# Every fifth streamed weight piece as two DMAs, of 120 and of 8 partitions

## The chip, the cores and the metric

The kernel runs on one core of a Trainium2 chip. The metric is the time of one execution on the device in microseconds; lower is better. All data are bf16, and sums of products are kept in fp32.

## What is computed

Two branches over the same input x (2048 tokens of 640), mixed by a gate for each token:

```python
g = sigmoid((x * gate_w).sum(-1, keepdims=True))
a = A(x, mem0, Wq, Wk, Wv, Wo, seg_len=32)
b = (gelu(x @ w_gate) * (x @ w_up)) @ w_down          # hidden size 1536
return g * a + (1 - g) * b

def A(x, mem0, Wq, Wk, Wv, Wo, seg_len):              # 32 heads of 192, memory of 8 rows
    mem = mem0
    for s in range(n_seg):                            # 64 segments of 32 tokens
        h = concat([mem, x[segment s]])               # 40 rows of 640
        q, k, v = h @ Wq, h @ Wk, h @ Wv              # for 32 heads
        p = softmax(mask(q @ k.T * scale))            # memory rows see all, tokens are causal
        o = (p @ v) @ Wo                              # 40 rows of 640
        mem = o[:8]                                   # goes into the next segment
        outs.append(o[8:])
    return concat(outs)
```

Branch A is a recurrence: segment s+1 cannot start its projections of the memory rows before segment s has ended. Wq, Wk and Wv have 640 x 6144 elements each, Wo has 6144 x 640.

## The kernel before

All work is written out, instruction by instruction, by a small scheduler of the kernel's own (`_Sched`). `S_.add(engine, fns, reads, writes, dma_sem)` puts an operation at the end of an engine's list and notes which regions of memory it reads and writes. From these regions `finalize` works out the semaphore waits: an operation waits for the last writer of what it reads, and for the writer and the readers of what it overwrites. The order on each engine is that of the calls. On TensorE (PE) an operation that needs more than one wait keeps one, and the others are put on the last matmuls of the operation before it (lines 171 to 186). Other engines issue the waits one after the other ahead of the operation (line 201).

The run has three stages. First the dense branch B for all tokens (lines 739 to 771), then the projections of those rows of all segments that do not depend on the memory (line 804, their results are stored to DRAM and read back segment by segment at line 831), then the 64 segments one after the other (`segment`), which take most of the time.

In a segment, PE goes through the list PROG: projections of Q and K (line 871) and of V (line 905) for four groups of eight heads, transposes (line 883), scores (lines 926 and 937), transposes of the softmax (971, 972), products with V (991, 993) and the output projection (line 1020). The weights are cut into *pieces*: a piece of Wq, Wk or Wv is 128 partitions x 1536 elements (3072 bytes in a row, 384 KB), a piece of Wo is 128 partitions x 2 x 640 elements (two rows of 1280 bytes, 320 KB).

All weights together do not fit into the on-chip memory. Most pieces are *resident*: they are loaded once (line 597). The others, 24 in each segment, are *streamed*: each segment loads them anew, spread evenly over the segment by a table of estimated costs. Streamed pieces go into a ring of five slots (B_RING = 5). `piece(seg, key)` is called for each piece in the order of use. For a streamed piece it calls `issue_ring`, which puts a DMA on the list of SyncE (SP), line 549. As the five slots are taken in turn, this DMA waits until the matmuls that read the slot's piece before have ended. Nothing else runs on SP's queue in the recurrent stage, so an issue that waits holds up the issues behind it. Each slot has its own semaphore (`ring0` to `ring4`), and each has one region of the scheduler, `r_ring[slot]`, over all 128 partitions.

The order of the streamed pieces in a segment is Q, K, V pieces first (15 of them), then nine of Wo. `done` is the place of a piece in this order, 0 to 23. The ACT queue issues the other transfers: one for each segment at line 831, and input and output rows once in four segments (line 640).

Of the kernel before, what the change touches and what calls it, by code (L numbers as in the profile page):

```python
# [221 lines left out]
def _build(nc, A_x, A_mem0, A_Wq, A_Wk, A_Wv, A_Wo, seg_len, w_gate, w_up, w_down,  # L222
# [27 lines left out]
    GQ = OW * 2  # L250
# [6 lines left out]
    S_ = _Sched(nc)  # L257
# [66 lines left out]
    ring_off = [j * GQ for j in range(B_RING)]  # L324
    o = wsA_base - wsB_total
# [6 lines left out]
    o = wsA_base  # L332
# [4 lines left out]
    o = ffn_base  # L337
# [4 lines left out]
    def bview(o, nbytes, plo=0, phi=128):  # L342
        return arena[plo:phi, o // 2:(o + nbytes) // 2]
# [4 lines left out]
    def sreg(o, nbytes, plo=0, phi=128):  # L348
        return Rg("sb", o, o + nbytes, plo, phi)
# [100 lines left out]
    def piece_src(key):  # L450
        if key[0] == 3:
            return Wo2[:, 2 * key[1]:2 * key[1] + 2, :]
        m, o_, k = key
        return (Wq2, Wk2, Wv2)[m][:, k, OW * o_:OW * (o_ + 1)]

    def piece_size(key):
        return GO if key[0] == 3 else GQ

    def piece_view(key, o):
        if key[0] == 3:  # L460
            return bview(o, GO).rearrange("p (c n) -> p c n", n=Dm)
        return bview(o, GQ)
# [55 lines left out]
    o = ring_bytes  # L518
# [9 lines left out]
    o = ring_bytes  # L528
# [5 lines left out]
    assert o <= wsA_base - wsB_total  # L534
    r_res = {key: sreg(o, piece_size(key)) for key, o in res_off.items()}
    r_ring = [sreg(o, GQ) for o in ring_off]
    order_index = {key: i for i, key in enumerate(order)}
    stream_pos = {order[i]: k for k, i in enumerate(stream_list)}
    stream_counter = [0]
# [4 lines left out]
    def issue_ring(seg, upto):  # L544
        done = issued.get(seg, 0)
        while done <= upto:
            key = order[stream_list[done]]
            slot = stream_counter[0] % B_RING
            S_.add("sp", lambda e, slot=slot, key=key: e.dma_start(piece_view(key, ring_off[slot]), piece_src(key)),
                   writes=[r_ring[slot]], dma_sem="ring%d" % slot, name="ring s%d p%d" % (seg, done))  # L550
            stream_counter[0] += 1
            ring_of[(seg, key)] = slot
            done += 1
        issued[seg] = done

    def piece(seg, key):
        oi = order_index[key]
        assert oi == last_req.get(seg, -1) + 1, "pieces must be consumed in `order`"
        last_req[seg] = oi
        if seg == 0:  # L560
            load_late(oi + LATE)
        if key in res_off:
            assert slot_class[key] != 1 or order_index[key] <= order_index[late[late_done[0] - 1]]
            return piece_view(key, res_off[key]), r_res[key]
        issue_ring(seg, stream_pos[key])
        slot = ring_of[(seg, key)]
        return piece_view(key, ring_off[slot]), r_ring[slot]
# [75 lines left out]
    def ffn_x_load(blk):  # L643
# [7 lines left out]
           writes=[r_gwr], dma_sem="gwr")  # L651
# [144 lines left out]
    for o_ in range(NOCT):  # L796
        st, rst_ = lst[o_ % 2], r_lst[o_ % 2]
        for m in range(2):
            gs = [left_piece((m, o_, k)) for k in range(KT)]
            for i in range(12):  # L800
# [6 lines left out]
                    name="left o%d m%d c%d" % (o_, m, i))  # L807
# [9 lines left out]
        for d in range(nd):  # L817
            lo, hi = d * NSEG // nd, (d + 1) * NSEG // nd
# [4 lines left out]
                name="left store")  # L823

    issue_ring(0, B_RING - 1)
    S_.add("pool", lambda e: e.memset(pl_sb, 0.0), writes=[r_p])
    S_.add("pool", lambda e: e.memset(Ks[64:128, 8:12, :], 0.0), writes=[r_Kz[0]])
# [251 lines left out]
    for s in range(NSEG):  # L1079
# [6 lines left out]
                ring=B_RING, arena_bytes=arena_bytes,  # L1086
# [25 lines left out]
def bass_gated_mix__memory_aug_recurrent_mem_tr__glu_gated_geglu__prompt_kernel(  # L1112
    nc,
    A_x,
    A_mem0,
    A_Wq,
    A_Wk,
    A_Wv,
    A_Wo,
    A_seg_len,  # L1120
    B_x,
    B_w_gate,
    B_w_up,
    B_w_down,
    gate_w,
    out,
):
    _build(nc, A_x, A_mem0, A_Wq, A_Wk, A_Wv, A_Wo, A_seg_len, B_w_gate, B_w_up, B_w_down, gate_w, out)
# [33 lines left out]
```

## Time and profile before

| | |
|---|---|
| time, median of 3 runs | 2227.48 us (2223.69 to 2227.95) |
| span of the profiled execution, first to last instruction | 2220.5 us |
| time of the profiled execution beside its span | the profile gives the span alone; the median of the runs is 7.0 us above it |
| mean granted TensorE clock | 0.986 |
| PE busy | 1912.3 us (86%) |
| VectorE / ScalarE / GpSimd busy | 943.6 / 799.7 / 273.6 us |
| DMA packets, bytes | 363257, 642.75 MB, 289 GB/s on average |
| HBM read | 618.74 MB |

How to read it: the time of a run is that of the whole execution, and the span is what the hardware profiler saw of it in one further execution. PE is TensorE's matmuls, PEld its weight loads, DVE VectorE, ACT ScalarE, POOL GpSimd, SP SyncE; a q behind the name (SPq) is the engine's sequencer, which issues DMAs and waits. "arena" is the one on-chip buffer in which all tiles lie, "ps" the accumulation banks. The chain of waits is followed back from the last instruction: at each step to what released it. "From issue to landing" of a DMA is the time from its issue on the queue to the last of its semaphore's increments. The 16 DMA engines' share of busy time is a mean over all of them.

### The profile page before, as it was taken

The page shows a single profiled execution, that of the slowest core. Times are in us where ns is not written, and L with a number is a line of the kernel's source. Part 1 is how long each engine was busy: PE and PEld are TensorE (multiplying, and loading weights), DVE is VectorE, ACT ScalarE, POOL GpSimd, SP SyncE. Part 2 cuts the span into 40 slices and gives each one's busy share as a digit, 9 for nine tenths or more (in the row PEclk, how much of TensorE's full clock was granted, in tenths as well). Part 3 has the DMA queues.
Part 4 walks back from the last instruction along what each step waited for, and adds up shares of the span by engine and source line. Part 5 has one row for each costly group of instructions (what it writes and reads, how often), then busy time and mean ns, then how long its engine had stood idle before and what let it go on. Part 6 is the DMA issues. An engine that isn't in the chain of part 4 may idle for free.

```text
span 2220.5 us, 94985 instructions
## 1 busy us (share of the span) xinstructions
PE 1912.3 (86%) x41834; PEld 1231.3 (55%) x41862; DVE 943.6 (42%) x3184; ACT 799.7 (36%) x2248; POOL 273.6 (12%) x1210
## 2 busy tenths in 40 slices
PE   7999958888888888888888888888888888888887
PEld 3544425555555555555565655555555655555655
DVE  2222223444444444444444444444444544444444
ACT  2222223334333333343333333333333334333333
POOL 0000001111111111111111111111111111111111
PEclk9999989999999999999999999999999999999999
DMA  9203579999999999999999999999999999999998
GB/s 370 88 13 112 150 236 331 322 303 316 301 318 307 324 303 311 305 316 312 319 320 311 316 300 320 306 313 310 320 302 321 309 322 311 315 315 316 310 309 278
DMA packets 363257, 642.75 MB, mean 289 GB/s; under 512 B 60498, under 2 KB 231770, under 8 KB 362842
## 3 DMA queue, kind: packets, MB, share of 16 engines
q1 hardware_dynamic: 311770, 601.01, 80.2%
q10 hardware_dynamic: 51072, 35.66, 5.4%
q8 instruction: 327, 5.36, 0.9%
q14 instruction: 88, 0.72, 0.1%
HBM read 618.74 MB, written 17.83 MB: 287 GB/s over the span
## 4 chain that ended last, share of the span: by engine, by line
PE 46%; DMA 32%; DVE 14%; ACT 3%; issue 3%; ACTq 2%; SPq 0%; DVEq 0%
PE ps L871 12%; DMA arena<-in_A_Wv_dram 10%; DMA arena<-in_A_Wo_dram 9%; PE ps L1020 9%; DMA arena<-in_A_Wk_dram 8%; PE ps L905 7%; DMA arena<-in_A_Wq_dram 4%; DVE arena L974 4%; PE ps L804 3%; PE ps L883 2%; PE ps L742 2%; PE ps L739 2%; ACTq L819 2%; PE ps L757 2%; DVE ps L954 2%
## 5 line engine op out<-in xcount | busy, mean ns | idle before, releaser
L871 PE MATMUL ps<-arena 128*32 128x384 bf16 x10240 | 488.1, 330 | 69.6 <-DMA arena<-in_A_Wk_dram 23.6
L1020 PE MATMUL ps<-arena 128*128 128x40 bf16 x15360 | 457.9, 180 | 64.8 <-DVE arena L1007 38.1
L1020 PEld LDWEIGHTS ps<-arena 128*128 128x128 bf16 x15360 | 428.9, 96 | 88.8 <-DVE arena L1007 49.5
L871 PEld LDWEIGHTS ps<-arena 128*32 128x32 bf16 x10240 | 247.1, 97 | 254.6 <-DMA arena<-in_A_Wk_dram 63.2
L905 PE MATMUL ps<-arena 128*32 128x384 bf16 x6400 | 324.4, 331 | 53.3 <-DMA arena<-in_A_Wv_dram 30.2
L877 ACT ACTIVATE arena<-ps 128x384 bf16<-128x384 f32 x512 | 249.8, 488 | 181.0 <-PE ps L871 105.1
L974 DVE TENSOR_TENSOR arena<-ps,arena 128x320 bf16<-128x320 bf16 x256 | 125.8, 491 | 387.0 <-PE ps L972 387.0
L835 POOL COPY arena<-arena 128x96 bf16<-128x96 bf16 x256 | 67.4, 263 | 1665.0 <-PE ps L937 1138.3
L956 ACT ACTIVATE ps<-ps 104x160 f32<-104x160 f32 x256 | 71.9, 281 | 494.5 <-DVE ps L954 494.5
L905 PEld LDWEIGHTS ps<-arena 128*32 128x32 bf16 x6400 | 144.6, 96 | 175.5 <-DMA arena<-in_A_Wv_dram 59.2
L883 PE MATMUL ps<-arena 128*128 128x128 bf16 x1536 | 175.9, 223 | 32.0 <-ACT arena L877 31.9
L1001 ACT ACTIVATE arena<-ps 128x320 bf16<-128x320 f32 x256 | 112.3, 439 | 215.4 <-PE ps L993 213.8
L991 PE MATMUL ps<-arena 128*128 128x160 bf16 (+1 forms) x768 | 130.5, 260 | 57.1 <-DVE arena L977 39.6
L916 ACT ACTIVATE arena<-ps 128x384 bf16<-128x384 f32 x256 | 125.6, 491 | 139.0 <-PE ps L905 138.7
L839 POOL COPY arena<-arena 64x32 bf16<-64x32 bf16 (+1 forms) x768 | 165.4, 215 | 47.3
L883 PEld LDWEIGHTS ps<-arena 128*128 128x128 bf16 x1536 | 88.1, 98 | 135.7 <-ACT arena L877 91.1
L952 DVE TENSOR_REDUCE arena<-ps 104x4 f32<-104x160 f32 x256 | 80.9, 316 | 149.3 <-PE ps L937 149.3
L894 ACT ACTIVATE arena<-ps 64x128 bf16<-64x128 bf16 x512 | 136.8, 267 | 6.3
L887 DVE COPY arena<-ps 128x384 bf16<-128x384 bf16 x256 | 89.4, 349 | 102.0 <-PE ps L883 102.0
L993 PE MATMUL ps<-arena 128*128 128x64 bf16 (+1 forms) x768 | 124.5, 202 | 4.0 <-ACT arena L877 4.0
L958 DVE TENSOR_REDUCE arena<-ps 104x4 f32<-104x160 f32 x256 | 83.1, 325 | 99.8 <-ACT ps L956 99.8
L991 PEld LDWEIGHTS ps<-arena 128*128 128x128 bf16 x768 | 72.3, 97 | 91.2 <-DVE arena L977 90.7
(81 smaller groups left out, 1886.3 us busy)
## 6 DMA issues: line engine op xcount, KB each, us to landing
arena<-in_A_Wo_dram SPq DMA_DIRECT2D x591, 320.0 KB, 4.7
arena<-in_A_Wv_dram SPq DMA_DIRECT2D x398, 384.0 KB, 5.2
arena<-in_A_Wk_dram SPq DMA_DIRECT2D x340, 384.0 KB, 5.3
arena<-in_A_Wq_dram SPq DMA_DIRECT2D x276, 384.0 KB, 5.0
left_qk_scratch<-arena ACTq DMA_DIRECT2D x16, 768.0 KB, 8.7
arena<-left_qk_scratch ACTq DMA_DIRECT2D x64, 192.0 KB, 4.6
arena<-in_A_x_dram SPq DMA_DIRECT2D x4, 640.0 KB, 15.0
ffn_b_scratch<-arena ACTq DMA_DIRECT2D x16, 160.0 KB, 1.8
```

The lines of the kernel that those rows point to most:

```text
L839: S_.add("pool", lambda e, a=a, b=b, lo=lo, hi=hi, sa=sa: e.tensor_copy(out=Ks[lo:hi, a:b, L:R], in_=stg[lo:hi, o, 1, sa:sa + b - a]), rea ...
L871: S_.add("pe", [lambda e, j=j, k=k, g_=g_: e.matmul(ps[32 * j:32 * j + 32, bank, 0:384], Hb[hb][:, k, 0:L], g_[:, 384 * j:384 * (j + 1)], ...
L877: S_.add("act", lambda e: e.activation(out=rows_sb, in_=ps[:, bank, 0:384], func=ACTF.Copy), reads=[r_ps[bank]], writes=[r_rows], name="ro ...
L883: S_.add("pe", [lambda e, c=c: e.transpose(pv[:, c * 128:(c + 1) * 128], rows_sb[:, c * 128:(c + 1) * 128], ident) for c in range(3)], rea ...
L894: S_.add("act", lambda e, a=a, lo=lo: e.activation(out=Ks[lo:lo + 64, a:a + 4, 0:L], in_=src[lo:lo + 64, 1], func=ACTF.Copy), reads=[r_ps[ ...
L905: return [lambda e, j=j: e.matmul(ps[32 * j:32 * j + 32, bk, 0:384], lhs, g_[:, 384 * j:384 * (j + 1)], start=(k == 0), stop=(k == KT - 1) ...
L916: S_.add("act", lambda e: e.activation(out=v_sb[o % NVB], in_=ps[:, bank, 0:384], func=ACTF.Copy), reads=[r_ps[bank]], writes=[r_v[o % NVB ...
L974: S_.add("dve", lambda e: e.tensor_tensor(out=PTm, in0=apx(pv[:, 512:616], [[64, 2], [0, 4], [1, R]]), in1=apx(mbd, [[0, 2], [1, 4], [0, R]]),
L991: return [lambda e: e.matmul(full, v[:, e0:e0 + 128], PTm[:, ia:ib], start=True, stop=False, skip_group_check=True), lambda e: e.matmul(pa ...
L993: lambda e: e.matmul(part, vl[:, e0:e0 + 128], PTl[:, ia:ib], start=False, stop=True, skip_group_check=True)]
L1001: S_.add("act", lambda e: e.activation(out=apx(u[:, 0, 0, :], [[2 * R, 2], [3 * R, 4], [1, R]]), in_=ps[:, A, 0:2 * W].rearrange("p (c t r ...
L1020: fns.append(lambda e, g_=g_, i=i, c=c, n=n, tl=tl, cc=cc, u=u: e.matmul(ps[:, OB, n * R:(n + 1) * R], g_[:, i, n * 128:(n + 1) * 128], u[ ...
```

## The change

Inside a segment, the streamed pieces whose place `done` leaves 2 when divided by 5 (the places 2, 7, 12, 17 and 22) are issued as two DMAs one after the other: partitions 0 to 119, and partitions 120 to 127. Each slot has two more regions for these parts, and one more semaphore (`ringb0` to `ringb4`) for the second part. The matmuls that use such a piece read the region of the whole slot, so they wait for both. The other pieces, the residents, and the pieces that the stage before the segments streams (line 585) are issued as before. In the 64 segments this makes 320 DMAs more.

```diff
     r_ring = [sreg(o, GQ) for o in ring_off]
+    r_ringp = [(sreg(o, GQ, 0, 120), sreg(o, GQ, 120, 128)) for o in ring_off]
...
             slot = stream_counter[0] % B_RING
-            S_.add("sp", lambda e, slot=slot, key=key: e.dma_start(piece_view(key, ring_off[slot]), piece_src(key)),
-                   writes=[r_ring[slot]], dma_sem="ring%d" % slot, name="ring s%d p%d" % (seg, done))
+            if done % 5 == 2:
+                parts = ((0, 120, r_ringp[slot][0]), (120, 128, r_ringp[slot][1]))
+            else:
+                parts = ((0, 128, r_ring[slot]),)
+            for lo, hi, rg in parts:
+                S_.add("sp", lambda e, slot=slot, key=key, lo=lo, hi=hi: e.dma_start(
+                    piece_view(key, ring_off[slot])[lo:hi], piece_src(key)[lo:hi]),
+                    writes=[rg], dma_sem=("ring%d" if lo == 0 else "ringb%d") % slot, name="ring s%d p%d" % (seg, done))
             stream_counter[0] += 1
```

## The prediction

> **What bounds the kernel now.** I read the page from the top: busy shares, DMA queues, chain of waits; then the longest pieces in order of time, the stages, the lines that issue the pieces, and the waits of PE and of SP.
>
> ```profile
> span 2220.5 us, 94985 instructions
> PE 1912.3 (86%) x41834; PEld 1231.3 (55%) x41862; DVE 943.6 (42%) x3184; ACT 799.7 (36%) x2248; POOL 273.6 (12%) x1210
> ...
> PE 46%; DMA 32%; DVE 14%; ACT 3%; issue 3%; ACTq 2%; SPq 0%; DVEq 0%
> PE ps L871 12%; DMA arena<-in_A_Wv_dram 10%; DMA arena<-in_A_Wo_dram 9%; PE ps L1020 9%; DMA arena<-in_A_Wk_dram 8%; PE ps L905 7%; DMA arena<-in_A_Wq_dram 4%; DVE arena L974 4%; PE ps L804 3%; PE ps L883 2%; PE ps L742 2%; PE ps L739 2%; ACTq L819 2%; PE ps L757 2%; DVE ps L954 2%
> ```
>
> PE is busy most of the time, but the chain that ended last runs through it for 46% only. 32% of it are DMAs, nearly all of them the four streams of weights. So neither is the bound alone: they take turns.
>
> ```profile
> 1000.00:1400.00 400.00, 346.94 (x8547) 233.31 (x8543) 181.19 (x638) 153.11 (x449) 55.87 (x248) 0.99 0.94 314
> 1400.00:1800.00 400.00, 344.73 (x8556) 231.47 (x8553) 184.43 (x654) 152.87 (x449) 56.85 (x252) 1.00 0.93 312
> ```
>
> Two stages of the recurrent loop: PE 346.94 of 400 us, the granted clock full, the 16 DMA engines 93 to 94% busy (the last two columns are their share and GB/s). There is little free time on either side.
>
> ```profile
> 1004.18 5.26 DMA arena<-in_A_Wq_dram
> 1009.44 0.04 issue
> 1009.49 1.32 PE ps L871 x28
> ```
>
> This is one leg of the chain: a piece is issued at 1004.18, lands 5.26 us later, and the projection that had waited for it starts at once. The issue itself had waited for PE to release the slot. Whatever lengthens the landing of such a piece lengthens the span.
>
> ```profile
> L549 SPq DMA_DIRECT2D arena<-in_A_Wo_dram x576: 367/368/1632, 334.2 to 2208.4; - x192
> L549 SPq DMA_DIRECT2D arena<-in_A_Wv_dram x384: 327/328/1191, 262.4 to 2197.9; - x192
> L549 SPq DMA_DIRECT2D arena<-in_A_Wk_dram x320: 327/328/2005, 262.0 to 2195.4; - x160
> L549 SPq DMA_DIRECT2D arena<-in_A_Wq_dram x256: 327/328/1382, 249.1 to 2194.6; - x128
> ...
> DMA to landing us min/median/max: 2.6/5.0/10.1
> ...
> L831 ACTq DMA_DIRECT2D arena<-left_qk_scratch x64: 320/326/2826, 310.0 to 2176.0; - x64
> ```
>
> L549 issues 1536 pieces in 64 segments, 24 in each. L831 issues once a segment, 63 times from 310.0 to 2176.0, so a segment takes 29.62 us and a piece comes every 1.23 us. With a landing of 5.0 us about four pieces (5.0/1.23) are in flight at a time, of the five that the ring holds: half of the landing time is queueing, since the shortest landing is 2.6 us.
>
> **The timed runs.** The page has no time of the profiled execution other than its span, 2220.5 us. The median of the runs is 2227.48, 7.0 us above it; I add changes of the span to the median. About 0.2% (4.5 us) is what a measurement of this kernel can tell from no change.
>
> **The change, part by part.** In each segment the pieces 2, 7, 12, 17 and 22 of 24 come as two DMAs: 320 in all, three of five being weights of Q, K or V (rows of 3072 bytes), two of Wo (two rows of 1280 bytes per partition). Bytes, matmuls and evictions stay the same. Three things are added.
>
> *First, rows on the DMA engines.* A 128-row piece is 8 rows on each of 16 engines. 120 rows do not divide by 16, and the 8 rows of the rest can fall on at most 8 engines. So some engines have between 8 rows (nothing added) and 9 (one added). A row's price is in the queue's row for the stage 600:2100:
>
> ```profile
> q1 hardware_dynamic: 233925, 448.32, 89.0%
> ```
>
> 89.0% of 16 engines over 1500 us are 21360 engine-us for 448.32 MB: 0.146 us for 3072 bytes and 0.122 for 2 x 1280. One row more in each split piece is then 3 x 0.146 + 2 x 0.122 = 0.68 us per segment on the engines that have it, 0.137 on average per split piece. Against 26.4 us (89.0% of 29.62) that these engines work on the ring in a segment, it is 2.6% more.
>
> How much of it reaches the end? If these engines bounded every segment, 64 x 0.68 = 44 us: the upper bound. By the chain it is less: 32% of 2220.5 are 711 us, or 142 legs of 5.0 us. In each leg four pieces are in flight, of which 4.05 x 5/24 = 0.84 are split, so a leg grows by 0.115 us where the engine that finishes last has a ninth row, and by nothing where it has not: between 0 and 16.4 us. No view tells which of the 16 finishes last; I take the middle, 8.2 us, since at most half of the engines have the ninth row and the profile singles none of them out.
>
> [...]
>
> *Second, issues on SP.* 320 more DMA instructions. The trace has small ones at the start:
>
> ```profile
> L649 SPq DMA_DIRECT2D arena<-in_A_mem_dram x1: 397/397/397, 0.8 to 0.8; - x1
> L650 SPq DMA_DIRECT2D arena<-in_gate_w_dram x1: 261/261/261, 1.3 to 1.3; - x1
> ```
>
> These carry 8 and 5 rows and take 0.40 and 0.26 us, about as long as a whole piece. 320 of them are 83 to 128 us of SP. What is queued behind each is the next piece's wait and issue, and behind that PE. What hides it:
>
> ```profile
> SPq L549 <- PE ps L905: 225.7, 183, 2.8
> SPq L549 <- PE ps L871: 215.1, 228, 2.1
> SPq L549 <- PE ps L1020: 176.7, 204, 2.1
> ...
> SPq L549 <- PE ps L883: 58.1, 83, 1.2
> ```
>
> SP waits for PE to release a slot, 1.23, 0.94, 0.87 and 0.70 us on average in these groups, which is longer than one issue. Where the cover fails, the next piece is issued up to 0.40 us late, 128 us at the very most. The chain gives SPq 0%, that is under 0.5% or 11 us for 1536 issues; a fifth more of them is worth about 2 us, and I take that. The second part also starts later than the first by one issue. With four pieces in flight it queues behind rows that are still to be moved, so I put that at nothing; without a queue the piece would land up to 0.40 us late, which for the 0.21 of legs that end on a split piece is 142 x 0.21 x 0.40 = 12 us.
>
> *Third, waits on PE.* A split piece has two semaphores, so PE waits twice, 320 waits more; one of them sits on the matmul before. What is queued behind is the matmul of the piece, which needs both parts anyway. The step "issue" after a landing is 0.04 us in the leg above: 320 x 0.04 = 13 us at most, nothing if the wait rides on an instruction that is issued anyway. I take nothing, since these waits resolve while PE still works on resident pieces in most cases.
>
> Sum: 8.2 + 2 + 0 = about 10 us. 2227.48 + 10 = **2237.5 us**, slower by 0.45%.
>
> **Rivals.** *Nothing measurable.* PE's own idle time for these pieces is small:
>
> ```profile
>   PE ps L871: 40.5, 70
>   PE ps L905: 30.2, 43
> ...
>   PE ps L1020: 23.2, 43
> ```
>
> That is 94 us in 156 waits of the 2220.5. If the split pieces are mostly those that land early, or if the engine with the ninth row has caught up before it matters, the time stays at 2227.5. For it: the 6 to 7% of free engine time, 1.9 us per segment, is more than 0.68. Against: 142 legs in the chain, so the landing decides often.
>
> *Faster.* 120 rows at 8 each fill 15 engines and leave one out. If that one is behind the others throughout now, it loses 5/24 of its ring rows, 0.84 pieces in each leg, and the pieces land when the next slowest is done. The gain has its limit in the 94 us above; a quarter of that, since the next engine takes over, is 23 us and gives 2204. From that point on, at which the left-out engine is more than the added 0.115 us per leg behind, this mechanism decides. For it: a further row of the queues,
>
> ```profile
> q8 instruction: 327, 5.36, 0.9%
> ```
>
> which is 14% of a single engine (0.9% of 16) if all the instruction loading ran on one. Against: nothing shows that it is one, nor which. [...]
>
> *Much slower.* If the 120 rows fall on only 8 engines (15 rows each, plus one), a split piece has 8 rows more on these than now: 8 x 0.68 = 5.5 us per segment against 1.9 us free, 3.6 x 64 = 230 us, or 2457. Half of that unevenness would give about 2280. Against: no row of before, since no ring piece of it has fewer than 128 rows. [...]
>
> **How the numbers follow.** Forecast (slower, up to the bound of 44 us): 0.68. Nothing measurable: 0.14. Faster: 0.11. Much slower: 0.07. So faster 0.11, same 0.14, slower 0.75. The range is from 2223 (the case of no change with its scatter; the fastest run shown is 2223.69) to 2272 (2227.5 plus the bound of 44 us); it leaves out the rivals on both sides, 0.18 together.
>
> **What would show it.** Right: landings of the ring pieces longer by about 0.1 us in the median, DMA waits of PE a little above 94 us, the DMA share at or above 0.93 in the two stages, SPq still near 0% of the chain, GB/s down by about 0.5%. The first step is wrong if the landings are unchanged or shorter, the second if SP's waits for PE vanish at many issues and SPq appears in the chain, the third if "issue" grows by more than 13 us. The whole is wrong if landings fall below 5.0 us and PE waits less for them (the left-out engine was the late one), or if landings of split pieces grow by a microsecond or more (uneven spread).

## The result and the profile after

The changed kernel takes 2400.13 us (median of 4 runs, 2388.53 to 2404.29) against 2225.64 us before (4 runs, 2223.69 to 2227.95): slower by 7.84%, with a 95% interval of 7.54 to 8.14%. My forecast was 2237.5 us and the range ended at 2272. The sign was right, and the size was off by a factor of seventeen: 175 us in place of 10.

The page after, its span, busy shares and chain:

```profile
span 2396.1 us, 95333 instructions
PE 1999.3 (83%) x41862; PEld 1244.6 (52%) x41862; DVE 943.5 (39%) x3184; ACT 800.1 (33%) x2248; POOL 273.6 (11%) x1210
...
DMA 52%; PE 34%; DVE 9%; ACTq 2%; issue 2%; ACT 2%; SPq 0%; DVEq 0%
DMA arena<-in_A_Wk_dram 19%; DMA arena<-in_A_Wv_dram 16%; DMA arena<-in_A_Wo_dram 15%; PE ps L878 7%; PE ps L912 6%; PE ps L1027 6%; PE ps L811 3%; DVE arena L981 3%; PE ps L749 2%; PE ps L746 2%; ACTq L826 2%; PE ps L764 2%; DMA arena<-in_A_Wq_dram 2%; PE ps L890 1%; PE ps L998 1%
```

The span grew by 175.6 us (2396.1 - 2220.5). The chain was 46% PE and 32% DMA; now it is 34% PE and 52% DMA. SPq is still at 0%, so the 320 further issues are not what is late.

The stages (the last two columns are the share of the 16 DMA engines and GB/s), and the ring's queue in the stage 600:2100 (packets, MB, share of 16 engines):

```profile
1000.00:1400.00 400.00, 331.83 (x7748) 213.11 (x7744) 162.97 (x576) 138.85 (x407) 50.07 (x222) 0.99 0.98 285
1400.00:1800.00 400.00, 333.36 (x7774) 215.34 (x7767) 167.21 (x592) 141.10 (x414) 52.35 (x232) 0.97 0.97 286
```

```profile
q1 hardware_dynamic: 216118, 410.37, 93.0%
```

The engines are busier than before (0.97 to 0.98 against 0.93 to 0.94) and move less (285 GB/s against 313). 93.0% of 16 engines over 1500 us are 22320 engine-us for 410.37 MB, which is 0.167 us for a row of 3072 bytes. Before it was 0.146. Each row became 14% dearer on average, though only one piece in five is split. The 8.85 MB of ring pieces in a segment (15 of 384 KB, nine of 320) take 8.85 x (22320/410.37 - 21360/448.32) / 16 = 3.7 us more on each engine. The line that runs once in a segment, now L838, gives a segment's length:

```profile
L838 ACTq DMA_DIRECT2D arena<-left_qk_scratch x64: 320/326/2748, 310.8 to 2347.9; - x64
```

It is (2347.9 - 310.8) / 63 = 32.33 us in place of 29.62, and 64 times 2.72 us are 174. So the 3.7 us account for nearly all of the loss: of free engine time there were about 2 us in a segment (7% of 29.62) and 0.8 us are left (2.5% of 32.33), and the other 2.5 us lengthen the segment.

Who waits for the ring, from the line that issues the pieces (now L555), and the landings of pieces of each size (KB, median us from issue to landing):

```profile
  PE ps L878: 100.0, 181
  PE ps L912: 56.9, 103
...
  PE ps L1027: 34.1, 84
...
DMA to landing us min/median/max: 2.9/5.7/11.8
```

```profile
arena<-in_A_Wv_dram SPq DMA_DIRECT2D x334, 384.0 KB, 6.0
...
arena<-in_A_Wk_dram SPq DMA_DIRECT2D x212, 384.0 KB, 5.9
arena<-in_A_Wk_dram SPq DMA_DIRECT2D x128, 360.0 KB, 6.0
```

The pieces of Wk before:

```profile
arena<-in_A_Wk_dram SPq DMA_DIRECT2D x340, 384.0 KB, 5.3
```

PE now waits 191 us for pieces, 94 before. The split pieces (360 KB is their 120-row part; the view gives no landing for the 8-row part) land about when the whole ones beside them do: all pieces in the queue are late together. That alone does not tell a ninth row on some engines from a higher price of every row, since in both cases the pieces queued behind would be late too. PE's busy time grew as well, by 87 us, with the same matmuls. A matmul of L871, now L878, takes 333 ns on average in place of 330 and the granted clock is 0.979 in place of 0.986, both changes under 1%, so that a slower PE explains at most 20 us of the 175.

### The profile page after: what moved, and what is told of

It is laid out like the page before. It is cut to its first block, busy times and chain, and to the rows that moved or that the text cites. A ratio compares the mean times of both kernels' runs of the same rounds, so it can differ in the third digit from the quotient of the medians.

```text
span 2396.1 us, 95333 instructions
## 1 busy us (share of the span) xinstructions
PE 1999.3 (83%) x41862; PEld 1244.6 (52%) x41862; DVE 943.5 (39%) x3184; ACT 800.1 (33%) x2248; POOL 273.6 (11%) x1210
## 4 chain that ended last, share of the span: by engine, by line
DMA 52%; PE 34%; DVE 9%; ACTq 2%; issue 2%; ACT 2%; SPq 0%; DVEq 0%
DMA arena<-in_A_Wk_dram 19%; DMA arena<-in_A_Wv_dram 16%; DMA arena<-in_A_Wo_dram 15%; PE ps L878 7%; PE ps L912 6%; PE ps L1027 6%; PE ps L811 3%; DVE arena L981 3%; PE ps L749 2%; PE ps L746 2%; ACTq L826 2%; PE ps L764 2%; DMA arena<-in_A_Wq_dram 2%; PE ps L890 1%; PE ps L998 1%
## 5 line engine op out<-in xcount | busy, mean ns | idle before, releaser
L878 PE MATMUL ps<-arena 128*32 128x384 bf16 x10240 | 535.6, 333 | 129.7 <-DMA arena<-in_A_Wk_dram 77.1
L1027 PE MATMUL ps<-arena 128*128 128x40 bf16 x15360 | 476.9, 180 | 73.6 <-DVE arena L1014 35.3
L1027 PEld LDWEIGHTS ps<-arena 128*128 128x128 bf16 x15360 | 438.3, 96 | 107.4 <-DMA arena<-in_A_Wo_dram 48.6
L878 PEld LDWEIGHTS ps<-arena 128*32 128x32 bf16 x10240 | 249.1, 97 | 365.7 <-DMA arena<-in_A_Wk_dram 158.6
L912 PE MATMUL ps<-arena 128*32 128x384 bf16 x6400 | 341.8, 332 | 75.8 <-DMA arena<-in_A_Wv_dram 56.9
L890 PEld LDWEIGHTS ps<-arena 128*128 128x128 bf16 x1536 | 88.5, 98 | 130.3 <-ACT arena L884 63.5
L998 PEld LDWEIGHTS ps<-arena 128*128 128x128 bf16 x768 | 72.8, 98 | 86.8 <-DVE arena L984 86.3
```

Of the source, the lines that this page charges most:

```text
L878: S_.add("pe", [lambda e, j=j, k=k, g_=g_: e.matmul(ps[32 * j:32 * j + 32, bank, 0:384], Hb[hb][:, k, 0:L], g_[:, 384 * j:384 * (j + 1)], ...
L890: S_.add("pe", [lambda e, c=c: e.transpose(pv[:, c * 128:(c + 1) * 128], rows_sb[:, c * 128:(c + 1) * 128], ident) for c in range(3)], rea ...
L912: return [lambda e, j=j: e.matmul(ps[32 * j:32 * j + 32, bk, 0:384], lhs, g_[:, 384 * j:384 * (j + 1)], start=(k == 0), stop=(k == KT - 1) ...
L998: return [lambda e: e.matmul(full, v[:, e0:e0 + 128], PTm[:, ia:ib], start=True, stop=False, skip_group_check=True), lambda e: e.matmul(pa ...
L1027: fns.append(lambda e, g_=g_, i=i, c=c, n=n, tl=tl, cc=cc, u=u: e.matmul(ps[:, OB, n * R:(n + 1) * R], g_[:, i, n * 128:(n + 1) * 128], u[ ...
```

## The experiments

Three theories stood after the result. *Count*: the second DMA, its issue and its waits. *Engines*: 15 and 8 engines, unevenly loaded. *Rows* (later *destination*): a part with fewer than 128 partitions gives its rows to the engines in such an order that engines meet at the destination. The diffs below are against the changed kernel and show only the lines that choose the pieces and their parts; the regions and semaphores are changed to match.

### Two halves of columns

```diff
-                parts = ((0, 120, r_ringp[slot][0]), (120, 128, r_ringp[slot][1]))
+                h = 1 if key[0] == 3 else OW // 2
+                rp = r_ringp[slot][1 if key[0] == 3 else 0]
+                parts = ((v[:, 0:h], src[:, 0:h], rp[0]), (v[:, h:2 * h], src[:, h:2 * h], rp[1]))
```

Here `v` and `src` are the whole piece in the ring and in DRAM, and `h` is half of its columns (for Wo, one of its two rows).

> The same pieces in two DMAs with a semaphore each, but cut by columns: both parts have all 128 partitions and half of each row. Three theories. Count: the second DMA, its issue and its waits cost the 175 us; then this kernel is at 2390 to 2410 us as well. Engines: the parts do not fill the 16 DMA engines evenly (15 and 8 of them); then this kernel stays within 10 us of 2226. Rows: any part with fewer than 128 partitions hands its rows to the engines in another way than a whole piece, so that engines get in each other's way at the destination; then this kernel stays within 10 us of 2226 too. The halved rows of a Q, K or V piece are more packets, for which I allow 10 us.

Measured: 2242.7 us, slower than before by 0.83% (0.51 to 1.16%), some 17 us. The second DMA and its waits are there as in the change, and nine tenths of the loss are gone. *Count* falls.

### 112 and 16 partitions

```diff
-                parts = ((0, 120, r_ringp[slot][0]), (120, 128, r_ringp[slot][1]))
+                parts = ((0, 112, r_ringp[slot][0]), (112, 128, r_ringp[slot][1]))
```

> The same pieces as 112 and 16 partitions, which both divide by 16: seven rows and one row on each engine. Engines: back within 15 us of 2226, since all 16 engines carry the same. Rows: still slower, by 60 to 200 us, since the rows of 112 partitions do not lie on the engines as those of 128 do. Count: 2390 to 2410 us.

Measured: 2342.34 us, slower by 5.31% (4.96 to 5.65%), 117 us. Both parts divide evenly by 16, and two thirds of the loss remain. An uneven load of the engines is not the main cause.

### Only the 120 partitions

```diff
-                parts = ((0, 120, r_ringp[slot][0]), (120, 128, r_ringp[slot][1]))
+                parts = ((0, 120, r_ringp[slot][0]),)
```

> The 8-partition part is left out (those partitions keep what the slot held before), the 120-partition part stays. Count: back to about 2226 us or a little below. Engines and rows: most of the 175 us stays, 2340 to 2400 us, since the 120-partition part is the one that holds the piece's bytes. If the 8-partition part is what costs (eight rows that all go to the same eight partitions), 2226 us.

Measured: 2371.68 us, slower by 6.55% (6.1 to 7.0%), 146 us. The last 8 partitions of such a piece are not loaded and keep what the slot held. With fewer bytes and no second DMA at all, most of the loss is there. It belongs to the 120-partition part. The second DMA and its 8 partitions account for the other 28 us.

### 112, 8 and 8 partitions

```diff
-                parts = ((0, 120, r_ringp[slot][0]), (120, 128, r_ringp[slot][1]))
+                parts = ((0, 112, r_ringp[slot][0]), (112, 120, r_ringp[slot][1]), (120, 128, r_ringp[slot][2]))
```

> The pieces as 112, 8 and 8 partitions: the first part fills 16 engines evenly, the two small parts go to eight engines each at the most. Against 112 and 16 it shows what small parts on few engines cost. Engines: a ninth row on eight engines as in my prediction, 10 to 30 us above 112 and 16. Rows: within 20 us of 112 and 16. If the 8-partition part is what costs, about twice the 175 us: 2500 us or more.

Measured: 2363.04 us, slower by 6.18% (5.91 to 6.44%), 138 us: 21 us above 112 and 16. The small parts have a price, but a small one. Taken alone this difference fits the figure of *Engines* (10 to 30 us) and is just outside that of *Rows* (within 20 us); it says nothing of the large part.

### Loads alone, by the number and the place of the partitions

```python
for j in range(12):                       # one stage; W = 6144 elements, 12288 bytes
    e.dma_start(t[0:120, j * W:(j + 1) * W], Q[0:120]).then_inc(sem[1], 16)
e.wait_ge(sem[1], 16 * 12)
```

Here `t` is the buffer that the rows land in, and `Q` is Wq as 640 rows of 6144 elements.

> Loads alone: nothing of the reference is computed. SyncE issues twelve stages of twelve DMAs each, one stage after the other; a DMA brings rows of 12288 bytes of Wq to so many partitions: 128, 120, 112, 96, 64, 32, 32 (source in two levels of 8 and 4), 16, 16 on every fourth partition, 8 (120 to 127), 8 on every fourth, 128 again. Engines: what counts is on how many of the 16 DMA engines the rows fall. Then 112, 96, 64, 32 and 16 rows run at the rate of 128 (some 370 GB/s, as in the first 60 us of the kernel before), 120 at 15/16 of it, 8 rows at half, and the choice of partitions changes nothing. Destination: rows of neighbouring partitions share a way into the on-chip memory, which passes no more than one engine moves (370/16 = 23 GB/s), so engines whose rows go to neighbours wait for each other. [...]

SP's timeline: the start of each stage's twelve issues, so that the difference of two starts is the time of a stage.

```profile
0.73 12.56 SPq L18 DMA_DIRECT2D land<-in_A_Wq_dram  x12
47.65 17.98 SPq L21 DMA_DIRECT2D land<-in_A_Wq_dram  x12
135.51 9.74 SPq L24 DMA_DIRECT2D land<-in_A_Wq_dram  x12
196.00 5.67 SPq L27 DMA_DIRECT2D land<-in_A_Wq_dram  x12
259.03 7.62 SPq L30 DMA_DIRECT2D land<-in_A_Wq_dram  x12
307.15 5.42 SPq L33 DMA_DIRECT2D land<-in_A_Wq_dram  x12
332.03 5.69 SPq L36 DMA_DIRECT2D land<-in_A_Wq_dram  x12
356.90 5.40 SPq L39 DMA_DIRECT2D land<-in_A_Wq_dram  x12
380.20 7.49 SPq L42 DMA_DIRECT2D land<-in_A_Wq_dram  x12
393.80 4.04 SPq L45 DMA_DIRECT2D land<-in_A_Wq_dram  x12
416.75 8.06 SPq L48 DMA_DIRECT2D land<-in_A_Wq_dram  x12
427.66 12.34 SPq L51 DMA_DIRECT2D land<-in_A_Wq_dram  x12
474.35 0.35 SPq L53 DMA_DIRECT2D out_dram<-land  x1
```

| partitions | us | GB/s |
|---|---|---|
| 128 | 46.9 | 402 |
| 120 | 87.9 | 201 |
| 112 | 60.5 | 273 |
| 96 | 63.0 | 225 |
| 64 | 48.1 | 196 |
| 32 | 24.9 | 190 |
| 16, neighbours / every fourth | 23.3 / 13.6 | 101 / 173 |
| 8, neighbours / every fourth | 23.0 / 10.9 | 51 / 108 |

The kernel ran once; its last stage repeats the first, and took 46.7 us. From the middle of the stages with 128, 120, 112 and 64 partitions, the mean busy share of the 16 engines and GB/s (last two columns; without a stage's start and last landing the rates are higher than in the table):

```profile
5.00:44.00 39.00, 0.00 (x0) 1.00 1.01 429
55.00:130.00 75.00, 0.00 (x0) 1.00 0.95 207
140.00:192.00 52.00, 0.00 (x0) 1.00 1.01 284
262.00:303.00 41.00, 0.00 (x0) 1.00 1.01 206
```

120 rows take nearly twice as long as 128. The engines are not idle meanwhile: 0.95 fits 15 of 16 engines busy throughout, and with 64 partitions all 16 are busy and move less than half of what they move to 128. So it is the time of each row that grows, which *Engines* has no room for. The pairs in the last two lines read the same rows of the source into the same number of partitions, and differ only in which partitions these are: spreading them gives 1.7 and 2.1 times the rate. So the limit is at the destination. The rates of 64, 32, 16 and 8 neighbours (196, 190, 101 and 51 GB/s) are about 8, 8, 4 and 2 times 25 GB/s, which is also what one engine moved on average with 128 partitions (402/16). 112 and 96 partitions lie between 64 and 128 (273 and 225 GB/s, against 196 and 402). Eight spread rows moved 108 GB/s; their twelve issues alone took 8.1 of the 10.9 us, so that pair says less than the other. The stage "32 rows, 8 x 4" ran as 32 rows did (24.9 us); its two levels are one range of rows, and it tells nothing if they are taken as one.

Some 15 busy engines moved 201 GB/s to 120 partitions and 16 moved 196 to 64, about what 8 engines move at 25 GB/s each. Engines that wait for each other in pairs at the destination would give this. That is my reading of the rates: no view shows how the rows are dealt out or where they meet.

### Loads alone, whole pieces with split ones among them

> Loads alone again, nothing of the reference is computed. Four stages of 45 pieces of 128 rows of 3072 bytes: whole; every fifth as 120 and 8 partitions; every fifth as 112 and 16; every fifth as two halves of columns. Then 120 rows of 12288 bytes in four ways: with the source in two levels of 10 and 12, of 12 and 10, of 8 and 15, and in one level. Destination: by the rates of the first loads run (402 GB/s for 128 rows, 201 for 120, 273 for 112, 101 for 16, 51 for 8) a split piece takes 0.85 to 1.33 us more as 120 and 8, and 0.3 to 0.8 more as 112 and 16; so 44 us for the first stage, 52 to 56 for the second, 47 to 51 for the third, 44 to 45 for the fourth. [...] Engines: the second, third and fourth stages take 44 to 46 us, and fewer engines are always slower.

The first five lines of SP's timeline; the fifth begins the stage after the four of 45 pieces.

```profile
0.73 35.42 SPq L19 DMA_DIRECT2D land<-in_A_Wq_dram  x45
47.83 44.77 SPq L23 DMA_DIRECT2D land<-in_A_Wq_dram  x54
106.84 40.16 SPq L27 DMA_DIRECT2D land<-in_A_Wq_dram  x54
159.83 37.57 SPq L31 DMA_DIRECT2D land<-in_A_Wq_dram  x54
208.05 23.29 SPq L34 DMA_DIRECT2D land<-in_A_Wq_dram  x12
```

45 whole pieces take 47.1 us; with every fifth as 120 and 8 they take 59.0, as 112 and 16 53.0, as halves of columns 48.2. Each stage took 2 to 3 us longer than I had given, but for each of the nine split pieces the excess over whole ones is 1.32, 0.65 and 0.12 us, and the first two lie in the ranges named (0.85 to 1.33 and 0.3 to 0.8). The 1.32 us are what 120 partitions (0.85 us above a whole piece) and 8 partitions (0.48 us) cost by the rates of loads alone, one after the other: the 8 rows are not hidden. In the kernel the three cost 0.55, 0.37 and 0.05 us for each of 320 pieces: the same order, and some four to six tenths of the price. A likely reason, not tested, is that the ring is on the chain for a part of the time only. The 120 rows in two levels of 10 and 12, of 12 and 10 and of 8 and 15, which were to change the number of engines, took 86 to 88 us, as 120 plain rows did (88.6). If the two levels are taken as one range of rows, these stages could not tell the theories apart.

### 64 and 64, 96 and 32 partitions

The edit is that of 112 and 16, with other numbers.

> The same pieces as 64 and 64 partitions. Destination: loads alone of 64 partitions ran at 196 GB/s, so a split Q, K or V piece takes 2.0 us in place of 0.98; as 112 and 16 (1.26 + 0.49) it had cost 117 us of the span and as 120 and 8 (1.83 + 0.48) 175 us, some 0.45 of what the rates give; so about 150 us here, 2360 to 2400. Engines: both halves fill 16 engines with four rows each; back to 2243 as with halves of columns, or below.

> The same pieces as 96 and 32 partitions. Destination: 96 partitions ran at 225 GB/s, 32 at 190, so 1.31 + 0.52 in place of 0.98 us: some 120 us, 2330 to 2370. Engines: six rows and two rows on each of 16 engines; about 2243.

Measured: 2433.37 us for 64 and 64, slower by 9.70% (9.17 to 10.22%), and 2356.72 us for 96 and 32, slower by 6.12% (5.64 to 6.61%). Splits that divide evenly by 16 cost 117 (112 and 16), 135 (96 and 32) and 211 us (64 and 64), in the order that the rates of loads alone give. The most even one is the worst. 64 and 64 lies 33 us above the range that I had given it, so one factor from rate to span is only a rough one. It does not even order all splits: by the same rates 120 and 8 is the dearest (1.83 + 0.48 = 2.31 us, against 2.0 for 64 and 64), and it cost 175 us, less than the 211. Why is open.

### Five pieces of Wo by columns

The kernel is that with halves of columns, and other pieces are cut:

```diff
-            if done % 5 == 2:
+            if done in (15, 17, 19, 21, 23):
```

> Five pieces of Wo in each segment (the places 15, 17, 19, 21 and 23) as two DMAs by columns: each part has all 128 partitions and one of the two rows of 1280 bytes, so there are as many packets as before and only the second DMA, its issue and its waits are added, 320 times. My prediction had 2 us for the issues and nothing for the waits: 2223 to 2232. If halves of columns cost 17 us through the second DMA, 2235 to 2250; the rest would be the halved rows.

Measured: 2228.72 us, slower by 0.30% (0.10 to 0.50%), about 7 us. This is what 320 further DMAs with their issues and waits cost, on these pieces, when the rows stay as they are. The ring's queue in the stage 600:2100 moves the bytes as before:

```profile
q1 hardware_dynamic: 237969, 448.25, 89.5%
```

### The order of the rows, with the number of engines changed by the source

Here the levels of the source cannot be merged, since a row is left out after each group:

```python
e.dma_start(t[0:120, j * W:(j + 1) * W], Q[0:130].rearrange("(a b) n -> a b n", a=10)[:, 0:12])  # its semaphore is left out here
```

> Loads alone, nothing of the reference is computed. Twelve loads in each of seven stages, rows of 12288 bytes. In six of them the source's rows come in groups with one row left out after each, so that its levels cannot be merged into one (in the second loads run, 120 rows took 86 to 89 us whatever the levels were, so they had been merged). 128 rows whole; 128 in 16 groups of 8; 120 in 15 groups of 8; 120 in 10 groups of 12; 64 in 16 groups of 4; 32 in 16 groups of 2; 32 in 8 groups of 4. Destination: 402 GB/s for the first and about 200 for 120 in 15 groups of 8. 120 in 10 groups of 12 then runs faster on fewer engines, if the number of groups sets the number of engines: each engine starts on a way of its own, 10 x 25 = 250 GB/s. 32 in 8 groups of 4 runs as fast as 32 in 16 groups of 2, about 190, with half as many engines. For 128 in 16 groups of 8: 402 if the good order belongs to 128 partitions, about 200 if it belongs to the plain shape. Engines: 120 in 10 groups is slower than in 15 by a third, 32 in 8 groups slower than in 16 by half.

```profile
0.73 12.63 SPq L18 DMA_DIRECT2D land<-in_A_Wq_dram  x12
47.72 18.65 SPq L21 DMA_DIRECT2D land<-in_A_Wq_dram  x12
136.96 22.45 SPq L24 DMA_DIRECT2D land<-in_A_Wq_dram  x12
227.07 32.21 SPq L27 DMA_DIRECT2D land<-in_A_Wq_dram  x12
296.20 7.68 SPq L30 DMA_DIRECT2D land<-in_A_Wq_dram  x12
344.06 7.57 SPq L33 DMA_DIRECT2D land<-in_A_Wq_dram  x12
369.39 9.03 SPq L36 DMA_DIRECT2D land<-in_A_Wq_dram  x12
394.81 0.36 SPq L38 DMA_DIRECT2D out_dram<-land  x1
```

128 plain rows take 47.0 us; the same number in 16 groups of 8 takes 89.2 (211 GB/s). Nothing is split there and nothing is uneven. 120 rows in 15 groups take 90.1 us, in 10 groups 69.1 (256 GB/s). The rows left out in the source are not the cause, since those 10 groups have them too, and 64 rows in 16 groups of 4 take 47.9 us, as 64 plain rows did (48.1). What is left for the 128 rows is the order in which they are dealt out, which no view shows. 32 rows take 25.3 us in 16 groups and 25.4 in 8. From the middle of the stages with 120 rows in 15 and in 10 groups and 32 rows in 8, share of the 16 engines and GB/s:

```profile
140.00:222.00 82.00, 0.00 (x0) 1.00 0.95 204
230.00:290.00 60.00, 0.00 (x0) 1.00 0.63 269
371.00:392.00 21.00, 0.00 (x0) 1.00 0.50 208
```

These shares fit 15, 10 and 8 of 16 engines, busy throughout. Ten engines are faster here than fifteen (256 GB/s against 196), and 32 rows on eight took as long as in 16 groups. Both results are what the destination theory had given (250 and 190), and the contrary of the engines theory.

### Every piece split

```diff
-            if done % 5 == 2:
+            if True:
```

> Every streamed piece of the segments as 120 and 8 partitions, not every fifth. Destination: 24 split pieces in a segment. In the second loads run a split piece of 384 KB cost 1.32 us more than a whole one (0.98), and one of 320 KB should cost in proportion, 1.1 more than 0.9. Then the transfers alone need 15 x 2.3 + 9 x 2.0 = 52 us of a segment, against 29.6 before, and set its length: 64 x 52 + 320 for the stages ahead = 3650 us; 2950 if the 8 partitions hide behind the 120 of the next piece (15 x 1.83 + 9 x 1.53 = 41 us). Engines, with a ninth row in every piece: 5 times what my prediction had, 2275 to 2310. If each split piece costs the same 0.55 us as with every fifth: 3100.

Measured: 2699.75 us, slower by 21.5% (19.7 to 23.3%), 473 us (two runs). That is 0.31 us for each of 1536 split pieces, less than the 0.55 of every fifth. It is above the range of *Engines* (2275 to 2310), but also below both figures for the destination theory (3650 and 2950) and below that of equal prices (3100). All three assume that the price of a split piece does not depend on its neighbours, which is what the last run looks at.

### Loads alone, five pieces in flight

> Loads alone, nothing of the reference is computed: 45 pieces of 128 rows of 3072 bytes in each of four stages. Whole pieces, every fifth as 120 and 8, and all as 120 and 8, each with five pieces in flight as in the ring; then all as 120 and 8 with no such limit. It asks why a split piece costs 0.55 us in the kernel with every fifth split and 0.31 with all, when it cost 1.32 us in loads alone with many in flight. If the costs of split pieces add up (1.32 us each, whatever the others are): 47, 59, 106 and 106 us. If pieces in flight together spread over the ways, so that a second split piece costs less than the first: 80 us or less for the third and fourth. If five in flight hide part of it behind the landing time: the second stage is less than 12 us above the first.

```profile
0.73 42.57 SPq L23 DMA_DIRECT2D land<-in_A_Wq_dram  x45
47.89 52.17 SPq L32 DMA_DIRECT2D land<-in_A_Wq_dram  x54
106.11 74.89 SPq L41 DMA_DIRECT2D land<-in_A_Wq_dram  x90
188.59 64.16 SPq L47 DMA_DIRECT2D land<-in_A_Wq_dram  x90
268.27 0.37 SPq L49 DMA_DIRECT2D out_dram<-land  x1
```

47.2 us for whole pieces, 58.2 with every fifth split, 82.5 and 79.7 with all split: 1.23 us for a split piece among whole ones, 0.78 and 0.72 where all are split. The costs do not add up (that would be 106 us); split pieces behind each other are cheaper. The third stage is somewhat above the 80 us that I had named for the theory of pieces spread over the ways, and the fourth just below it. The second stage is 11.1 us above the first, against 11.9 with many in flight, so the limit of five hides little. Of these prices 0.55/1.23 = 45% and 0.31/0.78 = 40% reach the kernel's end. Why neighbours of the same kind cost less was not tried further. That they fall out of step and meet less often is an idea only.

## Why the prediction was wrong

*First part, rows on the DMA engines.* This step failed. It counted rows (a ninth one on eight engines) and took their price, 0.146 us, as given. The price itself changed, to 0.167 us on average over the queue: by my reading of the rates, the rows of a part with fewer than 128 partitions are dealt out in such an order that engines wait for each other at the destination, which no view shows. In loads alone some 15 engines busy throughout moved 207 GB/s to 120 partitions, and 16 moved 429 to 128. The sign was right although the sum held nothing of this cost; that is luck. The upper bound of 44 us was a bound on the count of rows and no bound on the time, and it set the end of the range. The row that could have warned me was in the trace only as a missing one: I wrote under the rival "much slower" that no ring piece of before has fewer than 128 rows, and yet priced 120 rows by pieces of 128. A price with no row of its own needs a wider end. Twice the price, which is a figure chosen in hindsight, would have put 8 x 0.146 = 1.17 us on a split Q, K or V piece where the sum had one row, 0.146.

*The choice of the middle, 8.2 us,* had no basis in a row and turned out immaterial beside that.

*Second and third part, issues and waits.* Small, as forecast, though not as small: 2 us and nothing, against 7 us (2 to 11) for the same count of DMAs, issues and waits in the run with five pieces of Wo. SPq stayed at 0% of the chain.

*Hiding of the second part behind the queue.* This was put at nothing, and it held only in part. With the second DMA left out the loss was still 146 of 175 us, so that the second part is not the main cost. But it is worth the other 28 us, more than the 12 that I had given for a late start without a queue, and issues and waits explain about 7 of them. The rest goes with the 8 partitions' own transfer or its later start, which no run of the kernel separates; in loads alone that transfer was not hidden.

*The rival "nothing measurable"* fell because the 2 us of free engine time in a segment could not take in 3.7 us more work. *"Faster"* fell too: a left-out engine gained nothing that shows. *"Much slower"* had the right sign and size (2457, against 2400) by luck, with the wrong mechanism: I had the rows falling on eight engines. They need not be few: 64 and 64, whose loads alone kept all 16 engines busy, did worst of all the splits of every fifth piece. That engines wait for each other at the destination would be enough; it is a reading of the rates (206 GB/s from 16 busy engines to 64 partitions, 429 to 128), and no view shows it.

*The signs I named.* Landings were to grow by 0.1 us and grew by 0.7; PE's waits were to be a little above 94 us and are 191; GB/s were to fall by 0.5% and fell by 9%. The DMA share, to be at or above 0.93, is 0.97 to 0.98. "Issue" is 2% of the chain. None of the signs that were to show a wrong step appeared: the landings of the 120-partition parts grew by less than the microsecond named for an uneven spread (0.7 to 0.9 us; for Wk from 5.3 to 6.0).

## What to carry to other kernels

Load whole tiles of 128 partitions in one plain DMA. If a tile must come in parts, cut it by columns: here 320 cuts by columns cost 7 to 17 us and 320 cuts by partitions 117 to 211. A transfer that is cut does not pay alone, since it slows what else is in the queue (the whole pieces of Wk landed after 5.9 us in place of 5.3), so price it by a run of such loads among whole ones, not by counting its bytes or its engines. Here four to six tenths of that price reached the kernel's end.

## What the runs showed of the hardware

- A load to 120 partitions ran at half the rate of one to 128 (201 against 402 GB/s), with 12288 bytes in a row. Short rows are not the reason.
- 128 partitions alone did not give the full rate: with the source in 16 groups of 8 rows they ran at 211 GB/s, as plain rows at 402.
- Fewer engines can be faster: 120 rows in 10 groups at 256 GB/s with 0.63 of the engines busy, in 15 groups at 196 with 0.95.
- Busy engines are no sign of full rate: to 64 partitions all 16 were busy (1.01) and moved 206 GB/s, to 128 partitions 429.
- Which partitions, with all else the same: 16 rows at 101 GB/s to neighbours, at 173 to every fourth partition.
